# Turning the key-value product by VectorE and spreading it by small DMAs in a fused attention and FFN kernel

## The chip, the cores and the metric

The kernel runs on one core of a Trainium2 chip. The metric is the device time of one execution in microseconds, taken as the median of several runs. A profile of one execution shows what each engine did: TensorE (PE, with its weight loads as PEld), VectorE (DVE), ScalarE (ACT), GpSimd (POOL) and SyncE (SP), which issues most DMAs.

## The reference

Polynomial-sketch linear attention, then an FFN with a tanh-shrink activation. Four batches, four heads, 1088 tokens, head size 32.

```python
def phi(x):                                   # 32 -> 8 and 8 -> 64
    a = einsum('rd,bhsd->bhsr', S1, x)
    b = einsum('rd,bhsd->bhsr', S2, x)
    return einsum('bhsi,bhsj->bhsij', a, b).reshape(..., 64)
q_p, k_p = phi(q), phi(k)
kv  = einsum('bhsf,bhsd->bhfd', k_p, v)       # 64 x 32 per head
z   = sum(k_p, axis=2)
num = einsum('bhsf,bhfd->bhsd', q_p, kv)
den = einsum('bhsf,bhf->bhs', q_p, z)[..., None] + 1e-6
x   = (num / den) as (4352, 128)              # heads side by side
h   = x @ w_in                                # 128 -> 2048
out = (h - tanh(h)) @ w_out                   # 2048 -> 128
```

## The kernel before, in words

The attention works batch by batch. On the key side (`k_side`) the loaded keys are turned by VectorE (`kT`, L536), sketched by TensorE in 64x32 tiles (`ksk`, L581), turned back (`kab`, L593), multiplied out to 64 products per token (`w`, L648, on VectorE or GpSimd, three pieces a batch), and `kv_mm` (L663) sums products and values into one PSUM bank: `pv`, 128 partitions (head by 32 values) by 64 features. `gram` and `scmm` (L608, L618) give the denominators' weights.

The numerator (`num`, L818) wants kv the other way round, features on the partitions, and in all four partition quadrants, because it runs as 32x32 tiles: row quadrant g holds a quarter of the tokens, column quadrant h is a head, and the 64 features come in two halves x that are accumulated. `kv_tail` makes this so:

- `kvd`: a copy of pv to SBUF that repeats each half four times (128x256), on ScalarE or VectorE;
- `kvt`: two 128x128 transposes on TensorE (L681);
- `kvb`: a copy of the 128x256 result to SBUF, on ScalarE or VectorE.

Batch 0 has besides a quick path for its first 12 blocks (`kv_heads`, `q_heads`): a VectorE transpose of pv in 32x32 blocks (`kvh`, L691), a masked copy `kve` (L692) and two 128x128 matmuls (`num0.0`, `num0.1`, L737), whose casts to `xT` let the FFN begin.

The query side (`q_sketch` L759, `q_divide`, `q_piece`) does the like: sketch, transpose (`abc`, L764), denominators (`m`, `den`, `rd`, `aq`), products (`qp`, L802), transposes (`qpT`, L807), numerator, and two casts to `xT` (`x`).

The FFN takes `xT` in ten groups of columns (384, 352, 352, six of 512, 192). For each of 16 blocks of the hidden size: a matmul `h` (L923), a tanh on ScalarE (`th`, L927), for later groups an addition on VectorE (`dg`, L932), and a matmul `o` that sums into the output bank (L944). For the columns without `dg`, two matmuls with the product of both weights (`wch`, `wcl`, L948) supply the linear part. The output is turned by VectorE (`ot`, L953) and stored in four DMAs or more a group (`st`, L963). Three `ot` buffers take turns.

The order is written out by hand, or by a search: `TABLE` lists numbers of operations with a letter for the engine (v VectorE, a ScalarE, g GpSimd, t TensorE, s SyncE) and, after a colon, the buffer that a new value takes. Each engine runs its operations in that order and waits for semaphores of the operations that they depend on. F and f in the table are filler matmuls of 512 and 256 columns (L430, L429); they read a tile `zz` of zeros that VectorE fills first (L428). Operations marked `lock` take turns between VectorE and GpSimd. A large load waits until less than `CAP` bytes of earlier loads are on the way.

Of the kernel before, what the change touches and what calls it, by code (L numbers as in the profile page):

```python
# [19 lines left out]
CAP = 1.45e6  # L20
# [6 lines left out]
0v 15a 16s 18s 17s 56g 1g 10g 2g 14g 9g 13g 3g 6v 4v 5v 50v:0 12g 65g 58g 51v 54v 53v 52v 55g 7g 59g 19s 23s 22a 30s  # L27
21s F F F F F F F F F F F F 66t:0 84v 67t 69v:0 68t 70v F F F F f 71t:0 29s 20s 57g 8g 25s 72a:0 F f 73t 74a 24a 61g
27s 34s 64v 77v:0 76v:1 26s F F 85t:1 35s 78g:2 28s 107v 31s 75v 86v:0 87g:0 230a 88v:0 89v:0 90v:0 f 79t:0 80t 111t:0
81t 82v 33s F F F F F 238t:0 91v:0 92v:0 83g 229a 112v:1 42s 43s 32s 108a:0 95g:1 113g:0 96v:1 232g 40s 38s F f 237t  # L30
36s 39s 41s 114v:0 115v:0 f 109t f 93t:1 44s 37s 116g:0 239a 117g:0 119g:1 234g 231a f 97t:2 94v 110a:0 236g f 240t:0
124v:0 98a 45s 105s 100s 125v F 249t:1 250a:0 241t 253t:2 254a:1 251t:1 252a:2 233a 126t:0 255t:2 242v 48s 46s 257t:1
273t:0 128v:0 256a:3 281t:0 282t 283t 127v 279t:2 63g 129t:0 274a:4 259t:0 120v:0 258a:0 284t 261t:1 130v:0 118v 285t
280a:1 131t 243t:2 244t 99s 103s 101s 47s 102s 49s 104s 260a:2 262a:3 277t:0 263t:1 132v:0 121t:0 60g 133v 159v:0
278a:0 269t:0 160v 286t 136g:0 106s 264a:5 271t:1 235a 134v:1 123v 245t 122a 246t 270a:6 247a 161t:0 248v 135v:2
267t:0 265t:2 162v:1 272a:2 324t:1 266a:7 325a:8 62g 268a:9 137t:2 138t 139t 163v 169g:3 308t:1 170g:0 143v 140a:0
359t:0 309a:10 287t 288t 141t 360a:3 142a:0 316t:1 318t:2 317a:5 289t 275t:0 144t:0 178v 145v:0 146g:0 11g 147v:0
276a:7 319a:11 320t:1 290t 306t:0 291t 381t:2 292t 293t 321a:12 314t:1 307a:9 389t:0 382a:6 315a:2 294t 295t 304t:2
296t 390a:4 312t:1 305a:0 297t 298t 313a:7 299v:0 148v:0 332t:0 149v:0 164t:0 333a:1 165a:0 310t:2 311a:13 371t:1
336t:0 166t 367t:0 337t 328t:2 338t 339t 372a:0 167v:0 168v 322t:1 368a:14 329a:9 323a:10 179t:0 377t:0 330t:1 378a:13  # L40
150v:0 151v:0 326t:2 154g:1 327a:15 331a:16 340t 341t 342t 343t 152g:0 373t:0 374a:2 344t 387t:2 345t 180v:1 388a:5
334t:1 346t 335a:7 181g:0 347t 365t:0 348t 385t:2 366a:8 349t 386a:9 363t:1 350t 351t 352t 353t 369t:0 361t:2 155v
364a:1 153v 375t:1 376a:10 370a:7 362a:11 156t:0 383t:0 354v:1 379t:1 158a 391t:0 392t 182v:0 393t 157v 183v:0 394t
384a:12 430t:2 194v:0 380a:3 395t 418t:0 396t 431a:1 195v 414t:1 397t 444t:2 398t 399t 419a:8 400t 401t 436t:0 415a:0
402t 438t:1 403t 404t 184g:0 187v:0 213v 445a:2 432t:2 405t 406t 407t 408t 302s 437a:7 473t:0 439a:3 185g:1 433a:6
409v:2 428t:1 416t:2 171v:1 196t:0 474a:4 422t:0 446t:0 417a:5 429a:9 420t:2 434t:1 411s 172t:2 412s 197v:0 173t 198v
199t:0 174t 186v:0 189g:2 190v 205g:2 421a:10 424t:2 423a:0 435a:11 175a:0 200v:0 425a:12 447t 471t:0 472a:5 201t
440t:1 188v 176t 448t 426t:2 441a:13 357s 413s 410s 300s 489t:0 449t 450t 202v:0 203v 427a:8 490a:10 177v:0 442t:1
481t:2 214t:0 475t:0 451t 482a:0 443a:14 477t:2 206v:0 476a:15 452t 453t 487t:0 204v:1 478a:12 454t 499t:1 497t:2 455t
488a:8 456t 483t:0 457t 458t 215v:0 216v:0 217v:0 500a:9 218v:0 498a:16 469t:1 495t:2 459t 356s 219g:0 484a:1 485t:0  # L50
224v:0 225v:1 486a:6 470a:7 496a:11 191t:0 491t:0 222g:1 192v 220g:0 460t 493t:1 461t 462t 193a 524t:2 492a:17 463t
530t:0 223v 494a:3 479t:1 525a:13 464v:2 207t:0 465s 301s 531a:2 526v 208t 545t:2 501t:0 532v 536t:0 480a:14 527t:1
546a:18 221v 547v 537a:7 502t 503t 504t 538v 533t:2 505t 528a:5 506t 539t:0 529v 534a:4 507t 542t:1 540a:12 535v 508t
541v 543a:0 548t:2 509t 303s 510t 544v 560t:0 549a:1 511t 512t 554t:1 561a:14 550v 513t 562v 555a:6 551t:2 514t 552a:8
563t:0 515t 516t 556v 557t:1 517t 564a:10 518t 558a:3 553v 566t:2 567a:9 209t 565v 599t:0 600a:11 519v:0 572t:0 573t
559v 569t:1 570a:5 568v 602t:2 603a:13 358s 520s 467s 210v:0 601v 574t 523s 355s 575t 576t 571v 605t:0 577t 611t:1
578t 604v 606a:2 579t 608t:2 612a:4 607v 609a:0 211t 614t:0 615a:7 580t 613v 581t 617t:1 582t 610v 583t 616v 618a:12
620t:2 621a:1 584t 619v 623t:0 624a:6 212a:0 585t 586t 587t 588t 589t 626t:1 622v 625v 590v:1 635t:2 632t:0 226t:0
636a:3 627a:5 633a:8 637v 628v 641t:2 634v 629t:1 227a 647t:0 638t:0 648t 228v 649t 670t:0 671t 642a:9 639a:10 643v
675t:1 630a:2 644t:2 674t 640v 631v 650t 651t 652t 591s 466s 679t:2 593s 653t 678t 468s 672a:7 654t 655t 656t 657t  # L60
673v 682t:0 658t 683t 676a:8 677v 659t 686t:1 687t 660t 661t 645a:0 646v 702t:1 703t 680a:6 681v 691t:2 690t 522s 595s
521s 592s 684a:2 685v 704t 662t 688a:1 694t:0 695t 689v 692a:3 705t 663t 706t 699t:1 698t 597s 707t 708t 693v 730t:2
729t 664t 709t 710t 696a:5 697v 733t:0 734t 700a:4 701v 665v:0 596s 731a:6 598s 711t 712t 713t 669s 738t:1 737t 714t
715t 732v 735a:0 594s 736v 716t 717t 742t:2 741t 739a:1 718t 719t 740v 720v:2 745t:0 746t 667s 761t:0 762t 728s 750t:1
727s 743a:2 744v 749t 721s 668s 726s 722s 723s 666s 725s 747a:3 748v 763t 764t 765t 751a:4 753t:2 754t 766t 767t
757t:0 755a:0 758t 768t 769t 752v 724s 796t:1 770t 771t 772t 797t 756v 759a:1 798a:2 760v 773t 774t 784t:2 785t 786a:3
775t 791t:1 790t 776t 788t:0 792a:4 787t 803t:2 789a:0 802t 777t 778t 794t:1 793t 804a:5 808t:1 809t 799t:0 810t 800t
795a:1 801a:3 805t:2 806t 779v:1 780s 782s 807a:6 783s 811t 812t 813t 814t 815t 816t 781a 817t 818t 819t 820t 821t
822t 823t 824t 825t 826v:0 827s 829a 828s 830a
# [64 lines left out]
class _Prog:  # L134
# [40 lines left out]
    def plan(self, table, filler):  # L175
# [154 lines left out]
def bass_polysketch_attn__then__act_tanh_shrink_kernel(  # L330
# [24 lines left out]
    def pool(name, n, shape, dtype=FP32):  # L355
        return _singles([sb(name, shape, dtype) for _ in range(n)])
# [685 lines left out]
```

## Time and profile before

| | |
|---|---|
| median of 3 runs | 104.08 us (103.92 to 104.67) |
| profiled execution, its own time | 103.72 us |
| its span in the trace | 101.8 us |
| busy: PE, DVE, ACT, POOL | 97.0, 82.3, 80.1, 29.8 us |
| first FFN matmul starts | 17.10 us |
| FFN matmuls L923 and L944, share of the chain | 31% and 29% |
| fillers L430, share of the chain | 9% |
| loads from HBM | 8.95 MB, in the first third of the span |

The span is what the trace covers; some 1.9 us of the execution lie around it. A busy TensorE counts the modelled length of each matmul, which overlaps the next, so the distance between starts is what a matmul costs in a stream.

### The profile page before, as it was taken

How to read it: one execution, taken by the hardware profiler on the slowest of the kernel's cores; microseconds unless marked ns; L12 is line 12 of the kernel's file. 1: busy time of each engine (PE TensorE's matmuls, PEld its weight loads, DVE VectorE, ACT ScalarE, POOL GpSimd, SP SyncE). 2: the span in 40 equal slices, each digit the busy share in tenths (PEclk: the TensorE clock that was granted, in tenths of full speed). 3: DMA queues.
4: the chain of work that ended last, by engine and by line, in shares of the span. 5: the costliest groups of instructions: out<-in, count | busy, mean ns of one | idle time of the engine just before them, and what ended most of it. 6: DMA issues, size and time to landing. Idle time of an engine off the chain costs nothing.

```text
span 101.8 us, 3049 instructions
## 1 busy us (share of the span) xinstructions
PE 97.0 (95%) x1266; PEld 48.9 (48%) x1266; DVE 82.3 (81%) x148; ACT 80.1 (79%) x158; POOL 29.8 (29%) x50
## 2 busy tenths in 40 slices
PE   5999999999999999999999999999999999999960
PEld 2334666365744565554634454344453444444650
DVE  3449799699986996989998898688889788999530
ACT  0311257979799896998999799999979999989940
POOL 5130758963383292255501570000000000000000
PEclk9999999999999999999999999999999999999999
DMA  2898859999989300003400003106002640035445
GB/s 56 249 270 274 311 189 294 328 294 296 333 251 325 99 0 6 0 0 53 79 6 0 0 0 60 29 0 95 0 2 36 101 70 0 0 55 79 76 70 81
DMA packets 25917, 11.37 MB, mean 112 GB/s; under 512 B 19120, under 2 KB 23600, under 8 KB 25904
## 3 DMA queue, kind: packets, MB, share of 16 engines
q1 hardware_dynamic: 24528, 10.64, 40.6%
q10 hardware_dynamic: 1376, 0.54, 2.1%
q8 instruction: 10, 0.16, 0.7%
q14 instruction: 3, 0.02, 0.1%
HBM read 8.95 MB, written 2.23 MB: 110 GB/s over the span
## 4 chain that ended last, share of the span: by engine, by line
PE 95%; DVE 1%; ACT 0%; issue 0%
PE psb L923 31%; PE psb L944 29%; PE psb L430 9%; PE psb L818 6%; PE psb L663 5%; PE psb L581 3%; PE psb L948 3%; PE psb L759 3%; PE psb L737 1%; PE psb L608 1%; PE psb L901 1%; PE psb L429 1%; PE psb L681 1%; PE psb L706 1%; PE psb L887 1%; PE psb L618 1%
## 5 line engine op out<-in xcount | busy, mean ns | idle before, releaser
L927 ACT ACTIVATE th<-psb 128x512 bf16<-128x512 f32 (+3 forms) x135 | 70.3, 605 | 5.0 <-PE psb L923 4.3
L923 PE MATMUL psb<-xT,wi 128*128 128x512 bf16 (+3 forms) x160 | 47.3, 349 | 0.2 <-ACT th L927 0.2
L944 PE MATMUL psb<-th,wo 128*128 128x512 bf16 (+3 forms) x159 | 43.4, 347 | 0.0
L932 DVE TENSOR_TENSOR th<-psb,th 128x320 bf16<-128x320 f32 (+2 forms) x47 | 25.8, 558 | 4.5 <-ACT th L927 2.4
L923 PEld LDWEIGHTS psb<-xT,wi 128*128 128x128 bf16 x160 | 14.7, 98 | 22.8 <-ACT th L927 7.8
L944 PEld LDWEIGHTS psb<-th,wo 128*128 128x128 bf16 x159 | 15.3, 98 | 10.2 <-DVE ot L953 0.4
L802 POOL TENSOR_TENSOR qp<-ap,abc 128x768 f32<-128x768 f32 x8 | 12.0, 1511 | 6.9 <-DVE qp L802 5.4
L807 DVE STREAM_TRANSPOSE qpT<-qp 128x768 f32<-128x768 f32 x11 | 10.5, 962 | 0.2
L430 PE MATMUL psb<-zz 128*128 128x512 bf16 x26 | 9.3, 497 | 1.1 <-DVE zz L428 1.1
L648 POOL TENSOR_TENSOR w<-abk 128x768 f32<-128x768 f32 x5 | 7.5, 1517 | 8.4 <-DVE w L648 4.3
L953 DVE STREAM_TRANSPOSE ot<-psb 128x512 f32<-128x512 f32 (+3 forms) x10 | 6.2, 625 | 2.6 <-PE psb L944 2.6
L536 DVE STREAM_TRANSPOSE kT<-kL 128x576 f32<-128x576 f32 (+3 forms) x10 | 5.6, 600 | 1.4 <-DMA kL<-in_k_dram 1.4
L648 DVE TENSOR_TENSOR w<-abk 128x768 f32<-128x768 f32 x7 | 6.5, 947 | 0.1
L818 PE MATMUL psb<-qpT,kvb 32*32 32x288 f32 (+1 forms) x256 | 6.1, 392 | 0.0
L573 DVE STREAM_TRANSPOSE qT<-qL 128x1088 f32<-128x1088 f32 (+2 forms) x5 | 5.2, 1065 | 0.5 <-DMA qL<-in_q_dram 0.5
L663 PE MATMUL psb<-w,vL 128*32 128x64 f32 x288 | 5.4, 221 | 0.0
L764 DVE STREAM_TRANSPOSE abc<-psb 128x1152 f32<-128x1152 f32 (+1 forms) x4 | 5.0, 1262 | 0.4 <-PE psb L759 0.4
L663 PEld LDWEIGHTS psb<-w,vL 128*32 128x32 f32 x288 | 4.4, 110 | 2.0 <-issue 1.7
L430 PEld LDWEIGHTS psb<-zz 128*128 128x128 bf16 x26 | 2.8, 120 | 4.9 <-issue 3.1
L593 DVE STREAM_TRANSPOSE abk<-psb 128x288 f32<-128x288 f32 x8 | 3.4, 462 | 1.5 <-PE psb L581 1.5
L359 ACT ACT_TABLE_LOAD x1 | 1.3, 1283 | 4.2 <-DMA kL<-in_k_dram 4.2
L784 POOL TENSOR_TENSOR ap<-abc,rd 128x288 f32<-128x288 f32 (+1 forms) x3 | 1.9, 630 | 9.2 <-DVE rd L782 9.2
(90 smaller groups left out, 79.0 us busy)
## 6 DMA issues: line engine op xcount, KB each, us to landing
kL<-in_k_dram SPq DMA_DIRECT2D x8, 272.0 KB, 4.4
vL<-in_v_dram SPq DMA_DIRECT2D x15, 144.0 KB, 4.1
qL<-in_q_dram SPq DMA_DIRECT2D x6, 272.0 KB, 4.4
wo_f<-in_moe_w_out_dram SPq DMA_DIRECT2D x4, 256.0 KB, 4.1
out_dram<-ot SPq DMA_DIRECT2D x15, 64.0 KB, 2.0
wi_f<-in_moe_w_in_dram SPq DMA_DIRECT2D x3, 256.0 KB, 4.0
out_dram<-ot SPq DMA_DIRECT2D x8, 48.0 KB, 2.5
qL<-in_q_dram SPq DMA_DIRECT2D x2, 176.0 KB, 3.9
```

Of the source, the lines that this page charges most:

```text
L430: "F": lambda e, n: e.matmul(bank(3), zz.ap[:, 0:128], zz.ap[:, None, 128:384].to_broadcast([128, 2, 256]), start=True, stop=True)}, zop)
L536: P.add(_v(nb * 32 * (r1 - r0)), lambda e, n, e_=e_, nb=nb, r0=r0, r1=r1: e.transpose(kTv[b][r0].ap.rearrange("p (j u t r) -> p r j u t", ...
L648: P.add({**_v(768), **_gt(768)}, lambda e, n: e.tensor_tensor(out=wv.ap.rearrange("p (x i j) -> p x i j", i=8, j=8), in0=abh(0)[:, :, :, N ...
L663: i = e.matmul(pv[b].ap[h * 32:(h + 1) * 32, 0:64], vL[b][:, h, blk * 32:(blk + 1) * 32], wvs[b, p].ap[:, (bi * 4 + h) * 64:(bi * 4 + h + ...
L802: P.add({**_v(cn * 256), **_gt(cn * 256)}, lambda e, n, qp=qp, c0=c0, cn=cn: e.tensor_tensor(out=qp.ap[:, 0:cn * 256].rearrange("p (x i j) ...
L807: P.add(_v(cn * 256), lambda e, n, qp=qp, o0=o0, cn=cn: e.transpose(qt.ap[:, o0 * 256:(o0 + cn) * 256], qp.ap[:, 0:cn * 256]), r=[qp], w=[ ...
L818: i = e.matmul(psa4[h * 32:(h + 1) * 32, g, 0:nb * 32], kvb.ap[g * 32:(g + 1) * 32, x, h * 32:(h + 1) * 32], qq[g * 32:(g + 1) * 32, 0:nb, ...
L923: P.add(_mm(n_), lambda e, n, jb=jb, hv=hv: e.matmul(hv.ap[:, jb % m * 512:jb % m * 512 + n_], wi[jb // 4].ap[:, (jb % 4) * 128:(jb % 4 + ...
L927: act = P.add(_a(n_ * m), lambda e, n, hv=hv, th=th: e.activation(out=th.ap.rearrange("p (u x) -> p u x", u=m)[:, :, 0:n_], in_=hv.ap.rear ...
L932: P.add(_vp(gc * m), lambda e, n, hv=hv, th=th: e.tensor_tensor(out=th.ap.rearrange("p (u x) -> p u x", u=m)[:, :, 0:gc], in0=hv.ap.rearra ...
L944: fn = lambda e, n, x=x, st=st, sp_=sp_: e.matmul(ov.ap[:, 0:n_], wo[x // 4].ap[:, x % 4, :], ths[x][0].ap[:, ths[x][1] * 512:ths[x][1] * ...
L953: P.add(_vp(n_), lambda e, n: e.transpose(ot.ap[:, 0:n_], ov.ap[:, 0:n_]), r=[ov], w=[ot], name=f"ot{gi}")
```

## The change

1. `kv_tail` no longer copies, turns on TensorE and copies again. One VectorE instruction turns pv in 32x32 blocks straight into quadrant layout (`kvh1` to `kvh3`; batch 0 uses the transpose that its quick path has already). `kvb` of each batch has four slots; slot 0 is that transpose, in which quadrant h holds head h. Six DMAs from SBUF to SBUF a batch (`kvs`, 8 to 24 KB each) fill slots 1 to 3 with the same data, moved on by one, two and three quadrants. Tile (g, h) of the numerator reads slot (g - h) mod 4. A DMA may be issued by SyncE or ScalarE; in the new table ScalarE issues three of batch 0, SyncE all others.
2. Fillers read a constant of zeros that the program's preamble sets, spread by a zero step, so they depend on nothing. `zz` shrinks to 32 columns and is filled by GpSimd; only `gram0` reads it.
3. The 16 tiles of the numerator come in another order for each batch: diagonal (0), heads outermost as before (1), row quadrants outermost (2), heads outermost and reversed in the second half (3).
4. `CAP` rises from 1.45 to 2.0 million bytes.
5. `TABLE` is new on all engines. Among what moves: five of the `w` products from VectorE to GpSimd, `wqd` and a `wi` cast to GpSimd, both `qph` products to VectorE, the batch-0 q sketch behind the whole of `kvmm0`, `stt` ahead of the last `kT` of batch 0.

```diff
-CAP = 1.45e6
+CAP = 2.0e6
...
-    zz = sbv("zz", [128, 384], BF16)
-    zop = P.add({"vector": (1.0, 1.0)}, lambda e, n: e.memset(zz.ap[:, :], 0.0), w=[zz], name="zz")
-    filler = ({"f": ..., "F": ...}, zop)
+    zz = sbv("zz", [128, 32], BF16)
+    P.add({"vector": (120.0, 160.0), "gpsimd": (120.0, 160.0)}, lambda e, n: e.memset(zz.ap[:, :], 0.0), w=[zz], name="zz")
+    zc = nc.const_aps.tensor(0.0, [128, 1], FP32).bitcast(BF16)[:, 0:1]
+    fill = lambda n_: lambda e, n: e.matmul(bank(3)[:, 0:n_], zc.to_broadcast([128, 128]), zc.to_broadcast([128, n_]), start=True, stop=True)
+    filler = {"f": fill(256), "F": fill(512)}
...
     def kv_tail(b):
-        kvd, kvb = _Val(kvd_p), kvbv[b]
-        ...  kvd copy, kvt transposes, kvb copy
+        kvh, kvb = kvhv[b], kvbv[b]
+        if b:
+            P.add(_vp(64), lambda e, n: e.transpose(kvb.ap[:, 0, :], pv[b].ap[:, 0:64]), r=[pv[b]], w=[kvh], name=f"kvh{b}")
+        for r in range(1, H):
+            for j, (d0, s0, n_) in enumerate(((r * 32, 0, 128 - r * 32), (0, 128 - r * 32, r * 32))):
+                P.add({"sync": 480.0, "scalar": 400.0}, lambda e, n, r=r, d0=d0, s0=s0, n_=n_: e.dma_start(
+                    out=kvb.ap[d0:d0 + n_, r, :], in_=kvb.ap[s0:s0 + n_, 0, :]), r=[kvh], w=[kvb], dma=(n_ * 256, n_), name=f"kvs{b}.{r}{j}")
...
             for x in range(2):
-                for h in range(4):
-                    for g in range(4):
-                        i = e.matmul(psa4[h * 32:(h + 1) * 32, g, 0:nb * 32],
-                                     kvb.ap[g * 32:(g + 1) * 32, x, h * 32:(h + 1) * 32],
+                for i in range(16):
+                    u, w = i // 4, i % 4
+                    h, g = ((w, (u + w) % 4), (u, w), (w, u), (u if x == 0 else 3 - u, w if x == 0 else 3 - w))[b]
+                    r = e.matmul(psa4[h * 32:(h + 1) * 32, g, 0:nb * 32],
+                                 kvb.ap[g * 32:(g + 1) * 32, (g - h) % 4, x * 32:(x + 1) * 32],
```

In the new order, the entries of SyncE around batches 2 and 3 read (kvs: spreading DMAs, st: stores, lv: a load of v):

```text
st0.2, kvs2 x3, lv3.0, st0.3, kvs2, st2.3, kvs2, st2.0, kvs2, st1.3
kvs3 x2, st4.1, kvs3 x4, st4.3
```

More of the change, by code (lines that the diff above doesn't have):

```diff
@@ L32 @@
[L32 to L41, printed above, removed]
```

114 lines of the change are left out of this document (53 added, 61 removed).

## The prediction

> **What bounds the kernel now.** I read the page's slices and chain first, to see which engine sets the end, then the busy time by windows, then the chain in order of time, and last the timeline of the first 18 us.
>
> ```profile
> span 101.8 us, 3049 instructions
> ...
> PE   5999999999999999999999999999999999999960
> ...
> ACT  0311257979799896998999799999979999989940
> ...
> PE 95%; DVE 1%; ACT 0%; issue 0%
> ```
>
> ```profile
> 30.00:40.00 10.00, 9.96 (x147) 5.57 (x154) 8.86 (x14) 9.08 (x26) 4.70 (x6) 1.00 0.40 122
> ...
> 80.00:90.00 10.00, 10.00 (x50) 4.59 (x49) 9.27 (x13) 9.73 (x12) 0.00 (x0) 1.00 0.27 42
> ```
>
> After the stretch, the windows give busy time of PE, PEld, DVE, ACT, POOL. TensorE is busy in 9.96 and 10.00 of 10 us and carries 95% of the chain; ScalarE is second with 9.08 and 9.73. So from the first FFN matmul on, a microsecond of matmul work taken away is worth up to a microsecond, and VectorE or GpSimd work moved about is worth nothing unless it makes TensorE wait. The start is different: there TensorE's time is filler.
>
> ```profile
> 0.84 0.23 DVE zz L428
> 1.12 5.30 PE psb L430 x12
> 6.42 1.03 PE psb L581 x32
> 7.46 0.97 PE psb L430 x4
> ...
> 17.48 0.50 ACT th L927
> ...
> 22.48 1.22 PE psb L818 x59
> ...
> 27.95 0.22 PE psb L681 x2
> ...
> 34.45 0.70 PE psb L759 x32
> ...
> 71.41 0.22 PE psb L681 x2
> ...
> 71.94 0.27 PE psb L948 x2
> ...
> 75.27 1.53 PE psb L818 x63
> ...
> 78.20 1.08 PE psb L923 x5
> ...
> 98.41 0.38 DVE ot L953
> ```
>
> Columns: start, length, what. The twelve opening fillers take 5.30 us, 0.44 each; the four after the k sketch 0.24 each. So TensorE runs at half rate until about 7 us, and the sketch (L581) starts when the fillers end, not when its data is there:
>
> ```profile
> 4.72 0.24 DVE L542 STREAM_TRANSPOSE stt<-sin 128x64 f32<-128x64 f32 x1 [0.34 <-DMA sin<-in_S_dram]
> 4.89 0.76 DVE L536 STREAM_TRANSPOSE kT<-kL 128x256 f32<-128x256 f32 x2
> 5.23 0.24 POOL L545 TENSOR_TENSOR wab<-stt,mask 128x32 f32<-128x32 f32 x1
> 6.35 1.10 PE L581 MATMUL psb<-kT,wab 64*32 64x144 f32 x32
> 10.30 1.52 POOL L648 TENSOR_TENSOR w<-abk 128x768 f32<-128x768 f32 x1 [4.30 <-DVE w L648]
> 12.93 0.24 DVE L691 STREAM_TRANSPOSE kvh<-psb 128x64 f32<-128x64 f32 x1
> 13.60 1.49 SPq L465 DMA_DIRECT2D wo_f<-in_moe_w_out_dram  x3
> 17.10 0.34 PE L923 MATMUL psb<-xT,wi 128*128 128x384 bf16 x1
> ```
>
> Data is complete at 4.89 + 0.76 = 5.65; the sketch starts at 6.35.
>
> **The change part by part.** The sum is made against the profiled execution, 103.72 us (span 101.8, 1.9 around it). The runs' median, 104.08, stands 0.36 above it; I carry the difference over to the median.
>
> *Start.* A filler that reads a constant waits for no memset, so the first can start when zz's memset did, at 0.84, not 1.12: 0.28. The new order has eleven long fillers and a short one (half length) before the sketch, not twelve: 0.22 less at the half rate. Together 0.50, from 6.35 to 5.85. The lower bound on its start is data: with stt moved ahead of the last kT transpose, stt still waits for its load until 4.72, then 0.24 and half of 0.76 give 5.34, so the gain cannot pass 1.0; if something other than zz holds TensorE's first instruction, only 0.22 is left. I take 0.50. [...]
>
> From the sketch to the first FFN matmul I follow the new order by the rows. The sketch, the two products on VectorE, the one on GpSimd (1.52) and the last two parts of the kv product keep their distance: the batch-0 q sketch no longer stands between those parts, but two parts, not one, now follow GpSimd's product, and the two cancel. After the transposed kv (L691, 12.93) came qp, its transposes, kve, two numerators and two casts, up to 17.10; with both qp on VectorE and kve behind them I get the same 4.2 within 0.1. ScalarE also issues three small DMAs here, before the wiT copy; at 0.6 each (the load that ScalarE issues takes 607 ns, quoted below) they end before the copy's operands are there. So the 0.50 arrives at the first tanh, 17.48.
>
> *TensorE transposes.* kvt disappears for four batches. That of batch 0 lay among fillers: nothing. The three others (L681, the first and the last shown above) are 0.22 each on the bound engine: 0.66.
>
> ```profile
> L359 ACT COPY kvb<-psb 128x256 f32<-128x256 f32 x3 | 1.1, 382 | 0.0
> L359 ACT COPY kvd<-psb 128x256 f32<-128x256 f32 x3 | 1.1, 370 | 0.1
> L648 POOL TENSOR_TENSOR w<-abk 128x768 f32<-128x768 f32 x5 | 7.5, 1517 | 8.4 <-DVE w L648 4.3 <-DVE abk L593 3.3 <-DVE scx L628 0.8
> L648 DVE TENSOR_TENSOR w<-abk 128x768 f32<-128x768 f32 x7 | 6.5, 947 | 0.1
> L818 PE MATMUL psb<-qpT,kvb 32*32 32x288 f32 (+1 forms) x256 | 6.1, 392 | 0.0
> L932 DVE TENSOR_TENSOR th<-psb,th 128x320 bf16<-128x320 f32 (+2 forms) x47 | 25.8, 558 | 4.5 <-ACT th L927 2.4
> ```
>
> *Copies and products.* ScalarE loses 2.2 us of copies, VectorE two more copies; five of the 768-wide products move from VectorE (947 ns) to GpSimd (1517). Neither engine is on the chain; the cover is TensorE's FFN work. The place where the cover is thinnest is w1: its three products now run one after another on GpSimd behind qp and two casts, some 4.6 us, and the kv product of batch 1 stands about where the last is done. Between a gain of 0.2 (ScalarE late less often) and a loss of 0.5 I take 0.
>
> *Numerator order.* Batch 1 keeps its order; three change. The trace has two orders of 16 tiles: 32 matmuls of L818 take 1.53, 16 of L759 with rows outermost take 0.70. Two halves at 0.70 would be 0.13 better; two like the second half (0.83) 0.13 worse. Three batches: between -0.4 and +0.4; I take 0, as neither row is nearer. [...]
>
> *The spreading DMAs.* Six a batch, 8 to 24 KB, behind one VectorE transpose of 0.24, and the numerator waits for all six.
>
> ```profile
> out_dram<-ot SPq DMA_DIRECT2D x4, 8.0 KB, 2.3
> out_dram<-ot SPq DMA_DIRECT2D x4, 16.0 KB, 1.6
> ```
>
> ```profile
> L963 SPq DMA_DIRECT2D out_dram<-ot x45: 315/470/2009, 33.1 to 99.5; - x45
> ...
> DMA to landing us min/median/max: 1.5/1.9/3.5
> ```
>
> ```profile
> 76.23 6.19 SPq L963 DMA_DIRECT2D out_dram<-ot  x9
> ```
>
> ```profile
> L465 ACTq DMA_DIRECT2D vL<-in_v_dram x1: 607/607/607, 3.6 to 3.6; - x1
> ...
> DMA to landing us min/median/max: 2.8/4.0/5.3
> ```
>
> The last fence is of the loads (L465). No row shows an SBUF-to-SBUF DMA; the nearest are stores of the same size: 1.9 to land, and nine in succession take 6.19, of which one is the 2.01 maximum, so 0.52 each. Batch 0: the six go out by about 15, among loads that take at most 5.3 to land, so by 20.3; their numerator stood at 22.48 and moves to 21.9: hidden. SyncE stands still until the transposed kv is there, about 12.7, with wo, k2, q1 and v1 queued behind; before, the wo loads went out at 13.60, so nothing is lost, and the larger CAP lets one of them out ahead. Batch 1 has some 10 us. Batch 3: all six on SyncE with a store among them. After the kv product: a gate product on VectorE ahead (L932) 0.56, transpose 0.24, six issue steps 3.1, landing 1.9: 5.8, and some 0.2 for the product's last matmul to end: 6.0. TensorE has 29 matmuls of 0.216 (1.08 / 5) and a pair of 0.27 until the numerator: 6.5. Slack 0.5. Batch 2: 0.56, 0.24, nine issue steps (four other DMAs among the six) 4.7, landing 1.9: 7.4; cover 32 x 0.216 and a q sketch of 0.70: 7.6, and two small groups more. Slack 0.2 or a little over. I take 0, and keep as the upper end a 2.01 issue in each chain, 1.5 more than reckoned, so 1.0 and 1.3 of waiting; the lower end is 0, since nothing here can come out ahead of a copy that was already hidden.
>
> *Sum.* -0.50 - 0.66 = -1.16: 102.56 for the profiled execution, 102.9 for the median.
>
> **The rivals.** (1) The spreading is late for numerators 2 and 3, and the time is longer. Place: SyncE between kvh2, kvh3 and their last issue. For: nine steps in series, a slack of half a microsecond and less, a longest issue of 2.01 and a longest landing of 3.5. Against: medians. One such issue and landing in each chain cost 1.5 + 1.6 each, less the slacks: 2.6 + 2.9 = 5.5 at the worst; half of it, 2.7, gives 105.6. It is slower than no change by 1% from 2.2 us of waiting on, as the 1.16 has to be eaten first.
>
> (2) Half of the gain is lost in places of the new order: w1 late on GpSimd (0.5), one late numerator (0.5): 103.9. For: three dependent products in series, ScalarE at 9.7 of 10 at the end, where an earlier matmul only waits for a bank. Against: TensorE's full windows.
>
> (3) The change does not do what it says at the start: TensorE's first instruction is held by its own start, so the constant buys no time and only the shorter filler counts: -0.22 - 0.66, 103.2.
>
> [...]
>
> [...]
>
> **How the numbers follow.** A change of 1% (about 1.0 us) is what a measurement of this kernel tells from none: faster below 103.0, slower above 105.1. Forecast 102.9: 0.40, split by that border 0.30 and 0.10. Rival 1: 0.20, of which 0.15 slower and 0.05 between. Rival 2: 0.13, between. Rival 3: 0.07, between, but 0.02 of it below the border by scatter. Rival 4: 0.18. Rival 5 and unnamed mishaps: 0.02. Faster 0.50, same 0.33, slower 0.17. The forecast's own range is 102.1 to 103.6; for 8 in 10 it reaches to rival 4 below and into rival 1 above: 101.7 to 105.0.
>
> **What would show it.** Right: the sketch starts near 5.85 and the first tanh near 17.0; no L681; the numerators of batches 2 and 3 follow the matmul before them without a gap, with their last spreading DMA landed before; TensorE ends about 1.1 earlier than 98.4. Wrong: a weight load of the numerator that waits for kvb; a sketch still above 6.2; a numerator well off 1.53; windows after 30 us in which TensorE is busy for less than 9.9 of 10.

## The result and the profile after

The changed kernel is slower: 105.5 us median (104.8 to 107.91, 20 runs) against 104.06 (103.48 to 107.78, 20 runs) of the kernel before; ratio 1.013, 95% interval 1.0094 to 1.0166. The forecast was 102.9. The ratio leaves out the executions that lie some per cent above the others, which both kernels have. The profiled execution of the changed kernel took 106.16 us, with a span of 104.4 (before: 103.72 and 101.8), so it lies 0.66 above its median.

The page of the changed kernel, its slices and its chain:

```profile
PE   7989998999999998999999499999999999999940
...
PE 51%; SPq 22%; DMA 9%; ACT 6%; DVE 4%; issue 3%; DVEq 0%
PE psb L936 19%; PE psb L915 15%; SPq L462 11%; SPq L677 9%; PE psb L428 7%; DMA qL<-in_q_dram 5%; ACT th L919 5%; PE psb L810 5%; DMA kvb<-kvb 4%; PE psb L661 2%; PE psb L579 2%; SPq L955 2%; PE psb L940 1%; DVE ot L945 1%; DVE qT L571 1%
```

TensorE's share of the chain has fallen from 95% to 51%. SyncE's queue has 22% of it: its loads (L462, 11%) and, new, the spreading copies (L677, 9%), with another 4% for their landing. One slice of TensorE's row, the 23rd, has a 4 where there were nines.

The timeline of the changed kernel (start, length, engine, line, what; in brackets the idle time before it and what ended that):

```profile
5.77 1.05 PE L579 MATMUL psb<-kT,wab 64*32 64x144 f32 x32
...
17.01 0.87 ACT L919 ACTIVATE th<-psb 128x384 bf16<-128x384 f32 x2 [0.55 <-PE psb L915]
...
22.38 1.28 PE L810 MATMUL psb<-qpT,kvb 32*32 32x192 f32 x64
39.86 1.59 PE L810 MATMUL psb<-qpT,kvb 32*32 32x288 f32 x64 [0.31 <-DMA kvb<-kvb]
58.75 1.59 PE L810 MATMUL psb<-qpT,kvb 32*32 32x288 f32 x64 [1.53 <-DMA kvb<-kvb]
77.12 1.60 PE L810 MATMUL psb<-qpT,kvb 32*32 32x288 f32 x64
...
100.33 0.38 DVE L945 STREAM_TRANSPOSE ot<-psb 128x192 f32<-128x192 f32 x1 [1.26 <-PE psb L936]
```

The same numerators in the timeline of the kernel before:

```profile
22.41 1.28 PE L818 MATMUL psb<-qpT,kvb 32*32 32x192 f32 x64
...
39.13 1.60 PE L818 MATMUL psb<-qpT,kvb 32*32 32x288 f32 x64
...
56.54 1.60 PE L818 MATMUL psb<-qpT,kvb 32*32 32x288 f32 x64
75.20 1.60 PE L818 MATMUL psb<-qpT,kvb 32*32 32x288 f32 x64
```

Read as milestones, the two columns say where 2.6 us went. The sketch and the first tanh come 0.5 earlier, as forecast; by the numerator of batch 0 that lead is gone (22.38 against 22.41). From there to numerator 1 the changed kernel takes 17.48 against 16.72 (0.76 lost), to numerator 2 18.89 against 17.41 (1.48 lost, of which 1.53 is a wait for `kvb`), to numerator 3 18.37 against 18.66 (0.29 won), from there to the last `ot` 23.21 in both, and behind it 4.07 against 3.39 (0.68 lost).

A second profile of the changed kernel, taken further down, repeats this in part: numerator 0 stands 0.25 later than before, and then 0.19, 1.45 and 0.59 are lost at the same places and 0.28 won. So the 1.5 us at numerator 2 and the 0.6 at the end belong to the kernel; most of the 0.76 ahead of numerator 1, with its wait of 0.31 for `kvb`, belongs to that one execution.

The wait of 1.53 is what the windows show between 50 and 60 us; before, TensorE was busy for all of these 10 us. The changed kernel:

```profile
50.00:60.00 10.00, 8.42 (x127) 3.85 (x125) 7.51 (x11) 8.27 (x17) 7.40 (x7) 1.00 0.28 53
```

SyncE's part of the timeline, behind VectorE's transpose `kvh2`, shows why:

```profile
49.16 0.25 DVE L673 STREAM_TRANSPOSE kvb<-psb 128x64 f32<-128x64 f32 x1 [1.01 <-PE psb L661]
49.44 2.38 SPq L677 DMA_DIRECT2D kvb<-kvb  x3
51.86 0.60 SPq L462 DMA_DIRECT2D vL<-in_v_dram  x1
52.51 0.59 SPq L955 DMA_DIRECT2D out_dram<-ot  x1
53.14 0.53 SPq L677 DMA_DIRECT2D kvb<-kvb  x1
53.71 0.58 SPq L955 DMA_DIRECT2D out_dram<-ot  x1
54.34 1.95 SPq L677 DMA_DIRECT2D kvb<-kvb  x1
56.33 0.59 SPq L955 DMA_DIRECT2D out_dram<-ot  x1
56.95 0.49 SPq L677 DMA_DIRECT2D kvb<-kvb  x1
```

Ten issues one after another, the last at 56.95. The chain in order of time has the landing that follows it, up to numerator 2 at 58.75:

```profile
56.95 1.70 DMA kvb<-kvb
```

### The profile page after: what moved, and what is told of

It is laid out like the page before. It is cut to its first block, busy times and chain, and to the rows that moved or that the text cites. A ratio compares the mean times of both kernels' runs of the same rounds, so it can differ in the third digit from the quotient of the medians.

```text
span 104.4 us, 3053 instructions
## 1 busy us (share of the span) xinstructions
PE 94.9 (91%) x1245; PEld 47.6 (46%) x1255; DVE 77.5 (74%) x142; ACT 78.1 (75%) x152; POOL 37.9 (36%) x57
## 4 chain that ended last, share of the span: by engine, by line
PE 51%; SPq 22%; DMA 9%; ACT 6%; DVE 4%; issue 3%; DVEq 0%
PE psb L936 19%; PE psb L915 15%; SPq L462 11%; SPq L677 9%; PE psb L428 7%; DMA qL<-in_q_dram 5%; ACT th L919 5%; PE psb L810 5%; DMA kvb<-kvb 4%; PE psb L661 2%; PE psb L579 2%; SPq L955 2%; PE psb L940 1%; DVE ot L945 1%; DVE qT L571 1%
## 5 line engine op out<-in xcount | busy, mean ns | idle before, releaser
L915 PE MATMUL psb<-xT,wi 128*128 128x512 bf16 (+3 forms) x152 | 44.9, 347 | 0.5 <-issue 0.3
L924 DVE TENSOR_TENSOR th<-psb,th 128x192 bf16<-128x192 f32 (+2 forms) x48 | 26.3, 553 | 4.7 <-ACT th L919 2.5
L936 PEld LDWEIGHTS psb<-th,wo 128*128 128x128 bf16 x160 | 15.5, 99 | 10.3 <-DVE ot L945 0.2
L646 POOL TENSOR_TENSOR w<-abk 128x768 f32<-128x768 f32 x10 | 15.0, 1512 | 4.8 <-DVE w L646 3.3
L793 POOL TENSOR_TENSOR qp<-ap,abc 128x768 f32<-128x768 f32 x9 | 13.4, 1511 | 9.1 <-DVE qp L793 8.9
L428 PE MATMUL psb<-const-float32-0.0 128*128 128x512 bf16 (+1 forms) x29 | 9.9, 454 | 1.1 <-PEq L1019 0.8
L534 DVE STREAM_TRANSPOSE kT<-kL 128x512 f32<-128x512 f32 (+3 forms) x10 | 5.8, 600 | 1.6 <-DMA kL<-in_k_dram 1.6
L359 ACT CAST xT<-psb 128x192 bf16<-128x192 f32 (+3 forms) x6 | 2.9, 480 | 3.7 <-PE psb L810 3.4
L359 DVE CAST xT<-psb 128x576 bf16<-128x576 f32 (+2 forms) x4 | 2.8, 689 | 3.9 <-PE psb L810 3.9
L661 PE MATMUL psb<-w,vL 128*32 128x64 f32 x288 | 5.3, 221 | 0.0
L428 PEld LDWEIGHTS psb<-const-float32-0.0 128*128 128x128 bf16 x31 | 3.0, 114 | 4.7 <-issue 4.2
L661 PEld LDWEIGHTS psb<-w,vL 128*32 128x32 f32 x288 | 4.3, 110 | 1.9 <-issue 1.0
L810 PEld LDWEIGHTS psb<-qpT,kvb 32*32 32x32 f32 x256 | 3.3, 103 | 3.6 <-DVE qp L793 1.8
```

Of the source, the lines that this page charges most:

```text
L428: fill = lambda n_: lambda e, n: e.matmul(bank(3)[:, 0:n_], zc.to_broadcast([128, 128]), zc.to_broadcast([128, n_]), start=True, stop=True)
L646: P.add({**_v(768), **_gt(768)}, lambda e, n: e.tensor_tensor(out=wv.ap.rearrange("p (x i j) -> p x i j", i=8, j=8), in0=abh(0)[:, :, :, N ...
L661: i = e.matmul(pv[b].ap[h * 32:(h + 1) * 32, 0:64], vL[b][:, h, blk * 32:(blk + 1) * 32], wvs[b, p].ap[:, (bi * 4 + h) * 64:(bi * 4 + h + ...
L793: P.add({**_v(cn * 256), **_gt(cn * 256)}, lambda e, n, qp=qp, c0=c0, cn=cn: e.tensor_tensor(out=qp.ap[:, 0:cn * 256].rearrange("p (x i j) ...
L810: r = e.matmul(psa4[h * 32:(h + 1) * 32, g, 0:nb * 32], kvb.ap[g * 32:(g + 1) * 32, (g - h) % 4, x * 32:(x + 1) * 32], qq[g * 32:(g + 1) * ...
L915: P.add(_mm(n_), lambda e, n, jb=jb, hv=hv: e.matmul(hv.ap[:, jb % m * 512:jb % m * 512 + n_], wi[jb // 4].ap[:, (jb % 4) * 128:(jb % 4 + ...
```

## The experiments

Theory A at first: the loss is the place of the copies in SyncE's queue, with the rest of the gain lost in the new order. Its rival: copies cost wherever they stand, or the new order loses by itself. An edit of the order moves only what is named. All ratios are to the kernel before, on the same chip.

**The copies alone, in the old order.** Kernel before, with `kv_tail`, `kvb` and the numerator of the change:

```diff
-kvd1, kvt1, kvb1          (and 2, 3; batch 0 alike)
+kvh1, kvs1 x6             (kvs directly behind kvh in SyncE's queue)
```

> The kernel of before, in its own order and with its own loads and fillers, in which only the tail of kv is changed: the three-step tail (kvd, kvt, kvb) is gone for all batches, kvh stands where kvd stood, the six copies kvs stand right behind it (batch 0 split over SyncE and ScalarE as in the changed kernel, batches 1 to 3 all on SyncE), and the numerators read in the changed kernel's tile orders. Theory A (what costs is the place of the copies in SyncE's queue, behind stores and a load): six copies in a row take 6 x 0.6 us of issue and 2.4 us of landing, about 6.0 us behind kvh, and numerator 2 comes 7 us or more behind it, so nothing waits and the three kvt transposes are saved: 0.3 to 0.7 us faster than before, 103.4 to 103.8. Theory B (the copies are late wherever they stand): numerator 2 waits again for kvb, 1 us or more, and the time is 104.7 or above.

105.78 us, ratio 1.0144 (1.0089 to 1.0198): slower by as much as the whole change, which is theory B's number. So a loss of this size does not need the new order. Where it sits in this kernel is not told, since its profiled execution (107.69) is 1.9 above its median. Theory B's wait is not in that trace: no numerator waits for `kvb`, and numerators 1 to 3 are 36.06 apart (36.07 before). So the run does not show that the copies land too late here, and its loss stays open.

**The constant fillers alone.**

```diff
-fillers read zz, wait for its memset; 12 F, f
+fillers read the constant, wait for nothing; one f less
```

> The kernel of before in its own order; only the fillers multiply the built-in zero constant in place of the tile zz, and one half filler ahead of the first sketch is taken out. Nothing else differs. If the 0.5 us that the start gains lasts (theory A: it was lost on the way by the new order), the time is 103.5 to 103.7 against 104.06. If the stretch from 17 to 30 us is bound by something that does not start earlier, such as the loads (theory B), the first tanh comes 0.5 us earlier and the end does not: 104.0.

104.22 us, ratio 0.9999 (0.9969 to 1.003): nothing. Its timeline:

```profile
5.25 0.95 PE L580 MATMUL psb<-kT,wab 64*32 64x144 f32 x32
...
13.25 0.62 ACT L359 CAST wi<-wi_f 128x512 bf16<-128x512 f32 x1 [2.24 <-DMA wi_f<-in_moe_w_in_dram]
...
17.39 0.88 ACT L926 ACTIVATE th<-psb 128x384 bf16<-128x384 f32 x2 [0.43 <-PE psb L922]
```

The sketch starts 1.10 earlier than before (5.25 against 6.35), the first tanh 0.09 earlier (17.39 against 17.48). In between ScalarE waits 2.24 and 0.48 us for pieces of `w_in`. Theory B of this run holds in its number, and in its place more strongly than expected: already the first tanh is held, where the expectation had it 0.5 earlier.

**No copies at all**, in the changed kernel:

```diff
-for r in range(1, H): ... kvs
-kvb.ap[g * 32:(g + 1) * 32, (g - h) % 4, ...]
+kvb.ap[g * 32:(g + 1) * 32, 0, ...]
```

> The changed kernel without its 24 copies: the numerators read the tile kvh in place of all four rotated ones, so three of four head blocks get wrong operands; every matmul, shape and order stays. What the copies cost in all is the difference from the changed kernel. Theory A: the wait of 1.5 to 1.8 us at numerator 2 and 0.3 us at numerator 1 go, and with them SyncE's issues: 103.4 to 103.7 against 105.5. Theory B (the new order has slow places of its own, of which the wait at numerator 2 only hides one): 104.5 to 105.

103.58 us, ratio 0.9939 (0.9905 to 0.9972): theory A. The copies cost 1.9% in all, and all else in the change, with four kvt fewer, is worth 0.6%.

**The copies of batch 2 in front.**

```diff
-st0.2, kvs2 x3, lv3.0, st0.3, kvs2, st2.3, kvs2, st2.0, kvs2, st1.3
+kvs2 x6, ..., st0.2, lv3.0, st0.3, st2.3, st2.0, st1.3
```

> The changed kernel with one edit: in SyncE's queue the six copies of batch 2 stand in a row right behind the wait for kvh2, ahead of the load lv3.0 and of four stores that stood between them. Theory A: the last copy is issued about 3.6 us behind kvh2 in place of 7.8, lands near 55.5 us in place of 58.7, and numerator 2 follows TensorE without a gap near 57: 1.4 to 1.7 us faster than the changed kernel, 103.8 to 104.1. Theory B (the copies take as long as the queues and the memory let them, whatever their place): they land after 57.5 us and less than 0.7 us is won, 104.8 or above.

105.67 us, ratio 1.0104 (1.0062 to 1.0146): theory B's number, about 0.3 us under the changed kernel. The profiled execution (105.16) shows theory A's mechanism: the numerator no longer waits, 17.29 behind numerator 1 in place of 18.89. Then 0.4 us comes back, where TensorE waits for a load of v:

```profile
PE psb L661 <- DMA vL<-in_v_dram: 0.4, 1, 0.4
```

**Batch 0's copies behind the loads; and three batches moved.**

```diff
-lwo0, kvs0, lwo3, kvs0 x2, lwo1, lwo2, lk2.0
+lwo0, lwo3, lwo1, lwo2, kvs0 x3, lk2.0
```

> The changed kernel with one edit: in SyncE's queue the three copies of batch 0 stand behind the last load of w_out (lwo2) in place of among those loads, so that no load stands behind the wait for kvh0; the three copies on ScalarE stay. Theory A (the copies cost at the start, because a copy that waits for kvh0 at the head of SyncE's queue holds back the loads behind it): lwo3 to lk2 are issued up to 2 us earlier, as in the kernel without copies, the 25th tanh comes 0.5 us earlier or more, and the time is 104.5 to 105.0 against 105.5 to 105.7 of the changed kernel. Theory B (the copies cost by their issues on ScalarE, by their bytes, or only at numerator 2): 105.3 or above.

105.75 us, ratio 1.0117 (1.0062 to 1.0171): no gain that shows. Theory A of this run falls.

```diff
+kvs1 x6 behind lv2.2; kvs2 x6 behind kvh2; kvs0 as above
```

> The changed kernel with the copies of three batches moved in SyncE's queue: those of batch 0 behind the last load of w_out, those of batch 1 behind the last six loads that stood among them (lv2.2 the last), those of batch 2 in a row right behind kvh2. Theory A: no load waits behind a copy and no copy behind a store, so most of the 2.0 us that the copies cost by the run without them comes back: 103.6 to 104.3. Theory B (ScalarE's issues and the transfers themselves cost, or numerator 1 now waits for its later copies): 104.7 or above.

106.3 us, ratio 1.0152 (1.0103 to 1.02). A miss for theory A. Loads that are no longer held back behind copies of batches 0 and 1 are no gain that shows. It is no clean test, since lv3.0 now stands behind the copies of batch 2, as in the run with these in front.

**The kvt alone**, taken from the kernel before:

```diff
-P.add(_pe(260, 185.0), kvt, r=[kvd, ident], w=[pv[b]], ...)
-... kvb <- pv[b].ap[:, 0:256]
+... kvb <- kvd.ap
```

> The kernel of before without its four kvt transposes on TensorE: kvb is copied from kvd in place of from the transposed tile, so the numerators get the block as it was before the turn; all else stays. It prices the kvt alone. The sum of the prediction: three of them on the path at 0.22 us each, 0.66 us less: 103.5 to 103.8 against 104.06 to 104.33 (less 0.6 to 0.7 of it). The rival: TensorE has slack at those places, or something behind them sets the pace, and less than 0.3 us is won.

104.66 us against 104.66, ratio 0.9977 (0.9943 to 1.001): 0.24 us less by the ratio (0.6 less to 0.1 more), not 0.66, so the rival holds. Weight loads of TensorE around the place of `kvt3`, first in the kernel before, then without it:

```profile
71.03 0.35 PEld L681 LDWEIGHTS psb<-ident,kvd 128*128 128x128 f32 x2
71.54 0.10 PEld L923 LDWEIGHTS psb<-xT,wi 128*128 128x128 bf16 x1 [0.15 <-DVE th L932]
```

```profile
71.86 0.10 PEld L918 LDWEIGHTS psb<-xT,wi 128*128 128x128 bf16 x1 [0.49 <-DVE th L927]
```

Without the transposes the next FFN weight load waits 0.49 in place of 0.15 us for VectorE to give its bank back. From numerator 2 (56.86) to numerator 3 (75.52) this kernel takes 18.66, as before, and from numerator 0 to the last `ot` 75.98 against 76.00: in the traces all `kvt` together are worth 0.02. TensorE was busy for 59.96 of the 60 us from 31 to 91 in the kernel before, yet the cycle of first matmul, tanh, addition and bank had the slack: between 44 and 80 us its FFN weight loads wait 8.1 us for tanh and addition before, 9.0 without `kvt`.

**The changed kernel again**, unaltered:

> The changed kernel, unaltered, for a second profile on the chip of the other three. All theories: 105.3 to 105.8. If the 1.95 us issue ahead of numerator 2 was chance, the wait of TensorE at numerator 2 is near 0.5 us in this profile in place of 1.5 to 1.8, and what it is behind the kernel of before by then is the larger part of the loss; if it belongs to the order, the wait is 1.2 us or more again.

105.98 us, ratio 1.0137 (1.009 to 1.0185). Its numerator 2, and the issues of batch 2's copies in this profile (count, then least, median and longest ns):

```profile
58.43 1.59 PE L810 MATMUL psb<-qpT,kvb 32*32 32x288 f32 x64 [1.50 <-DMA kvb<-kvb]
```

```profile
L677 SPq DMA_DIRECT2D kvb<-kvb x6: 492/596/1891, 49.2 to 56.6; - x6
```

The long issue is no chance: it comes in both executions (1.95, 1.89), and so does the wait (1.53, 1.50). The traces of two other runs with this stretch of the queue unaltered have it at the same copy (batch 0's copies late: 1.98; the lower limit of loads, below: 1.96).

**Batch 2's copies and lv3.0 in front.**

```diff
-st0.2, kvs2 x3, lv3.0, st0.3, kvs2, st2.3, kvs2, st2.0, kvs2, st1.3
+lv3.0, kvs2 x6, ..., st0.2, st0.3, st2.3, st2.0, st1.3
```

> The changed kernel with one edit: the load lv3.0 and then the six copies of batch 2 in a row stand ahead of the stores that stood among them (the earlier run with the six copies alone in front lost 0.47 us again, because lv3.0 was pushed behind stores and the kv matmuls of batch 3 waited for it). Theory A (the wait at numerator 2 is 1.57 us in every execution, and it is the queue's order alone): from the 73rd to the 79th tanh 4.1 us in place of 5.7, from the 79th to the last 38.0, and the time falls by 1.4 to 1.6 us to 104.0 to 104.4, level with the kernel before. Theory B (what is won there is given back elsewhere, as the run with the copies alone in front showed in its median): 105.0 or above.

104.51 us, ratio 1.0004 (0.9967 to 1.0041): theory A, a little above its 104.0 to 104.4. By the ratios the order of one queue is worth 1.3%, and the kernel is level with before. Its timeline:

```profile
49.56 3.88 SPq L677 DMA_DIRECT2D kvb<-kvb  x6
53.49 4.71 SPq L955 DMA_DIRECT2D out_dram<-ot  x7
58.24 0.60 SPq L462 DMA_DIRECT2D vL<-in_v_dram  x1
...
57.27 1.60 PE L810 MATMUL psb<-qpT,kvb 32*32 32x288 f32 x64
60.83 0.88 PE L661 MATMUL psb<-w,vL 128*32 128x64 f32 x48 [0.34 <-DMA vL<-in_v_dram]
```

The numerator waits no more. But the kv product of batch 3 (L661) waits 0.34 us for v, though lv3.0 is out early: the late one is another, lv3.2, issued at 58.24 behind seven stores. What the expectation says of lv3.0 was wrong.

From numerator 1 to numerator 3 the traces take 36.07 us before, 37.26 and 37.24 in the two executions of the changed kernel, 36.14 with the copies alone in front and 36.07 here. So the place of the copies is worth 1.1 to 1.2 us in this stretch, and moving lv3.0 as well adds nothing that the traces show. Why the ratios of these two runs lie 1.0% apart (1.0104, 1.0004) is open; they were measured on different chips.

**The limit of loads in flight**, each way:

```diff
-CAP = 2.0e6      (changed kernel)
+CAP = 1.45e6
```

> The changed kernel with one number changed: at most 1.45 MB of loads in flight as before, in place of 2.0 MB; same order, same copies. Theory A (with more in flight the pieces of w_in share the memory with loads that are needed later, land 1 to 2.5 us later than before, and the second half of the first tanhs waits for them): the last piece of w_in lands near 14 to 15 us in place of 15 to 17, the 25th tanh comes 0.3 to 0.7 us earlier against the first, and the time is 104.8 to 105.3. Theory B (the limit does not matter there, or later loads now come late in turn): 105.5 or above.

```diff
-CAP = 1.45e6     (kernel before)
+CAP = 2.0e6
```

> The kernel of before with one number changed: 2.0 MB of loads in flight in place of 1.45. Theory A (more in flight delays the pieces of w_in): the last piece lands 1 us later or more, the first 24 tanhs take longer, and the time is 0.3 to 0.8 us above before. Theory B (the loss from 17 to 31 us belongs to the new order alone): within 0.2 us of before.

The changed kernel with 1.45 MB: 105.24 us, ratio 1.0062 (1.0026 to 1.0099), 0.7% under the changed kernel by the ratios, whose intervals just touch. The kernel before with 2.0 MB: 105.15 us, ratio 1.0062 (1.0023 to 1.0102). Theory A both times: the limit is worth about as much in either order. The loads of `w_in` on the pages of before, before with 2.0 MB, the changed kernel, and that with 1.45 MB (last number: us to landing):

```profile
wi_f<-in_moe_w_in_dram SPq DMA_DIRECT2D x3, 256.0 KB, 4.0
```

```profile
wi_f<-in_moe_w_in_dram SPq DMA_DIRECT2D x3, 256.0 KB, 4.8
```

```profile
wi_f<-in_moe_w_in_dram SPq DMA_DIRECT2D x3, 256.0 KB, 5.5
```

```profile
wi_f<-in_moe_w_in_dram SPq DMA_DIRECT2D x3, 256.0 KB, 4.3
```

The fourth piece, which ScalarE issues, takes 4.0, 5.9, 6.7 and 4.3. With the limit at 2.0 MB these loads take 0.8 to 2.4 us longer than at 1.45, and the ones that are needed first pay. How they pay is in the traces of the changed kernel, first with 2.0 MB, then with 1.45:

```profile
15.63 0.61 POOL L359 CAST wi<-wi_f 128x512 bf16<-128x512 f32 x1 [1.18 <-DMA wi_f<-in_moe_w_in_dram]
16.83 0.38 DVE L770 TENSOR_REDUCE den<-m 128x24 f32<-128x216 f32 x1 [0.81 <-POOL m L767]
18.23 0.19 PEld L579 LDWEIGHTS psb<-kT,wab 64*32 64x32 f32 x16 [0.55 <-DVE kT L534]
```

```profile
14.09 0.61 POOL L359 CAST wi<-wi_f 128x512 bf16<-128x512 f32 x1
15.84 0.38 DVE L770 TENSOR_REDUCE den<-m 128x24 f32<-128x216 f32 x1
17.40 0.18 PEld L579 LDWEIGHTS psb<-kT,wab 64*32 64x32 f32 x16 [0.17 <-DVE kT L534]
```

In the new order GpSimd casts the late piece and only then makes `m`; VectorE's `den` waits for `m`, `kT` stands behind `den`, and TensorE's sketch of batch 1 waits for `kT`. Numerator 0 stands at 22.38 with 2.0 MB and at 21.41 with 1.45 (22.41 before). The lower limit has its own price later: with it VectorE's `qT` waits for a load of q between 28 and 38 us.

```profile
DVE qT L571 <- DMA qL<-in_q_dram: 1.0, 1, 1.0
```

**Three edits together, and two limits.**

```diff
+lv3.0, kvs2 x6 in front; CAP = 1.45e6; st8.0 issued by ScalarE
```

> The changed kernel with three edits: lv3.0 and the six copies of batch 2 in a row ahead of the stores, 1.45 MB in flight, and one store of the last but one group (st8.0) issued by ScalarE in place of SyncE, so that SyncE has one issue less ahead of the last two stores. If the three act apart: 1.5 us less from the copies, 0 to 0.7 from the loads, 0.3 from the end: 103.2 to 103.9, faster than before by 0 to 0.8%. If the loads' limit gains nothing and the end stays: 104.2.

104.32 us, ratio 0.9965 (0.9929 to 1.0002): above the 103.2 to 103.9 of the expectation. The sum of the single prices by their ratios (1.3% and 0.7%) lies just inside the interval, so that they add up is neither shown nor excluded.

The second edit, on top of the moved load, copies and store:

```diff
-left = CAP - o.dma[0]
+left = (1.45e6 if o.name[:3] in ('lk0', 'lk1', 'lq0', 'lv0', 'lwi', 'lwo') else CAP) - o.dma[0]
```

> The changed kernel with lv3.0 and the six copies of batch 2 ahead of the stores, st8.0 issued by ScalarE, and the lower limit of 1.45 MB in flight for batch 0's loads, the weights and k of batch 1 alone; the later loads keep 2.0 MB. Theory A (the higher limit hurts the pieces of w_in only, the lower limit hurts q of batches 2 and 3 only): the first tanh near 16.6 us, no wait for q near 30 us, and the time is 0.6 to 1.0 us under the version with the higher limit: 103.3 to 103.8. Theory B (the early lead is lost again whatever the limit, since the stretch up to 36 us is bound by the loads' bytes): 104.2 or above.

104.18 us, ratio 1.0002 (0.9961 to 1.0044): theory B. By its median it lies 0.36 under before on its chip, by the ratio level: the two limits add nothing that can be told from none.

**Which copies carry the rest.** From the kernel with two limits: batch 0's copies behind lwo2, no copies in batch 0, no copies at all.

```diff
+kvs0 x3 of SyncE behind lwo2
```

> The kernel with two limits, in which besides SyncE's three copies of batch 0 stand behind the last load of w_out. Theory A (copies at the head of the queue that wait for kvh0 hold back loads that are needed by 30 us): 0.2 to 0.5 us faster than with them among the loads. Theory B (with the limit the loads are held back anyway): no difference within 0.3 us.

```diff
-for r in range(1, H):
+for r in range(1, H) if b else ():
```

> The kernel with two limits without the six copies of batch 0; its third numerator reads kvh for all four rotations, so part of batch 0's output is computed from the wrong operands, with the same matmuls in the same order. The difference from the kernel with them is the price of batch 0's copies. Theory A (that is where the 0.65 us sits, by SyncE's and ScalarE's issues at 12.5 to 16 us): 0.4 to 0.7 us faster. Theory B: within 0.2 us.

```diff
-for r in range(1, H): ... kvs
```

> The kernel with two limits without any of the 24 copies (every numerator reads kvh for all four rotations; same matmuls, same order): what is left if spreading cost nothing. By the run without copies and the higher limit (0.994 of before) and 0.4 to 0.7 us for the limit: 102.8 to 103.4. Theory A (batch 0's copies carry the price): within 0.2 us of the kernel that leaves out those alone. Theory B (copies of batches 1 to 3 carry it, by loads that stand behind copies of batch 1): 0.4 us or more below it.

Ratios 0.9988 (0.9948 to 1.0028), 1.0005 (0.9964 to 1.0047) and 0.9884 (0.9829 to 0.9939): theory B each time. Batch 0's copies cost nothing that shows; those of the other batches still cost 1.2%. In the run without batch 0's the kv product of batch 3 waits for lv3.2 as well, longer (1.07 us). From numerator 1 to 3 its trace takes 36.80 us, against 35.68 without any copies: there the whole price is that wait.

**The late load of v in front, and batch 1's copies behind the loads.**

```diff
+kvs1, lv3.0, lv3.2, then the stores and kvs2
```

> The kernel with two limits, in which both late loads of v of batch 3 (lv3.0 and lv3.2) stand right behind the copies of batch 1 in SyncE's queue, ahead of the first stores and of the copies of batch 2. Theory A (what is left of the copies' price is that load, which they push behind 57 us): TensorE no longer waits for v near 59 us, from the 73rd to the 85th tanh 7.3 us in every profile, and the time is 0.4 to 0.8 us under the kernel with two limits: 103.4 to 103.8, ratio 0.992 to 0.996. Theory B (the price sits in batch 1): no change beyond 0.2 us.

103.54 us, ratio 0.9962 (0.992 to 1.0003). Theory A: the wait is gone, and by the ratios about a third of the 1.2% with it, though the intervals overlap. From numerator 1 to 3 the trace takes 35.66, as without copies.

```profile
58.99 0.88 PE L661 MATMUL psb<-w,vL 128*32 128x64 f32 x48
```

```diff
+lv2.3, lv3.1, lk3.0, lv2.1, lk3.1, lv2.2, then kvs1 x6, lv3.0, lv3.2
```

> The kernel c1 with the six copies of batch 1 behind the last of the six loads that stood among them (lv2.2). Theory A: those loads are needed late and the copies of batch 1 land in time either way: within 0.3 us of c1. Theory B (loads that wait behind kvh1 cost): all loads are issued by 29 us in place of 36, and 0.3 to 0.6 us more is won. If numerator 1 then waits for its copies, 0.3 us or more is lost.

103.64 us, ratio 0.9958 (0.9922 to 0.9994): the same as the run before it, theory A, so loads behind batch 1's copies cost nothing that shows. It is the one version with copies whose interval lies under 1, and it does so by 0.0006, as the best of several: by the ratios, with the queue and the limit put right, it is 0.4% faster than the kernel before and 1.7% faster than the changed one. What is left between it and the run without copies (0.9884; the intervals overlap) is not settled; it is not in the stretch from numerator 1 to 3 (35.67 and 35.68).

The 0.68 that the changed kernel loses behind its last `ot` is not the copies' doing: the two traces without copies have 4.02 and 3.97 there, the kernel before 3.39 and that without `kvt` 3.27. It belongs to the new order; which of its moves makes it is open.

## Why the prediction was wrong

*Start, -0.50.* The numbers came out: sketch at 5.77 (forecast 5.85), first tanh at 17.01 (17.0). The first filler starts at 0.77, not 1.12, as reckoned. That the rest agrees is in part luck. The kernel without `kvt` has the start of before, and yet its sketch is 0.60 earlier than in the trace before and its first tanh 0.47 later (17.95):

```profile
1.12 4.50 PE L430 MATMUL psb<-zz 128*128 128x512 bf16 x12 [1.12 <-DVE zz L428]
5.75 0.95 PE L581 MATMUL psb<-kT,wab 64*32 64x144 f32 x32
```

The same twelve fillers take 4.50 in one execution and 5.30 in another, so only some 0.50 of the 1.10 of the fillers' run is theirs. That the clock makes the fillers slow, as "half rate" may be read, is not shown: 0.44 and 0.24 each are measured, and the windows have a granted clock of 1.00 from the start. In the second profile of the changed kernel the first tanh stands at 17.29.

The lead was worth nothing. The step that failed is that the sketch, its products and the numerators were followed to the first matmul, and not the casts of `w_in`, which wait for their loads. In the changed kernel the lead reaches the first tanh and is gone 1.2 us later, when the sketch of batch 1 starts (18.24, before 18.29), by the cast that waits 1.18 us; with the lower limit it lasts to numerator 0. The fillers alone leave the end where it was (ratio 0.9999 with a sketch 1.10 earlier). Rival 4, a time below the forecast, has 0.18 in the chances and sets the lower end of the 8-in-10 range, 101.7; no run shows a term that leads there: the lead of the start was worth nothing, and the numerators of batches 1 to 3 take 1.59 to 1.60 as before.

*Transposes, -0.66.* The step that failed is the rule that TensorE's busy time is worth up to its length because windows are full and TensorE has 95% of the chain. Measured 0.24 us, with 0 inside the interval, and in the trace 0: the next weight load waited for its bank instead (0.49 us in place of 0.15). The profile before had the row for it, weight loads that wait for VectorE's `th` (6.4 us in all):

```profile
L923 PEld LDWEIGHTS psb<-xT,wi 128*128 128x128 bf16 x160 | 14.7, 98 | 22.8 <-ACT th L927 7.8 <-DVE th L932 6.4 <-ACT xT L359 0.5
```

*The spreading DMAs, 0.* The step that failed is that the long issue was taken out of the row of stores (nine in 6.19) before the step was reckoned, and then left to the upper end: 0 where the prediction's own upper end for batch 2 was 1.3. Measured is a wait of 1.5. Reckoned for batch 2: nine issue steps of 0.52, 4.7. Measured: 49.44 to 56.95, 7.5, that is about 0.6 a step (the median of L677 is 596 ns) and two long ones: one among the first three, which take 2.38 where 1.8 would do, and the one of 1.95. At 0.62 from start to start nine steps would put the last issue at 55.0 and its landing at 56.7; TensorE is ready at 57.2 (58.75 less the wait). So by this estimate the slack was larger than reckoned, the step of 0.6 alone would have fitted into it, and the two long issues, 1.9 us more than plain ones, make the wait. Batch 3 had a slack and kept it: its numerator follows without a gap. Rival 1 had the place and the mechanism. That its 105.6 lies beside the measured 105.5 is luck: it halves waits at two numerators, where there was one wait, whole, and it counts the 1.16 as won, which was not. The landing, 1.9, was right where no load is on the way (1.7 to 1.8 in batch 3). Batch 0 was hidden, as forecast, though its copies (4.1 to 5.0) landed later than any store (4.0 at most in this profile):

```profile
L677 SPq DMA_DIRECT2D kvb<-kvb x3: 557/617/1157, 12.7 to 14.8; - x3
L677 ACTq DMA_DIRECT2D kvb<-kvb x3: 534/612/617, 12.7 to 13.9; - x3
DMA to landing us min/median/max: 4.1/4.6/5.0
...
L677 SPq DMA_DIRECT2D kvb<-kvb x6: 537/586/598, 70.9 to 74.6; - x6
DMA to landing us min/median/max: 1.7/1.8/1.8
```

These are the changed kernel's copies of batch 0, among loads, and of batch 3, among stores.

*CAP and the cast on GpSimd.* The prediction names the limit once, as something that lets a load out ahead. It costs 0.6 to 0.7% in either order, and in the new one it takes the lead of the start with it. No term of the sum had it, and no rival.

*The load behind the copies.* The prediction counted the copies' delay and not that of the loads and stores behind them: lv3.2 came late for the kv product of batch 3 as soon as the first wait was removed.

*Numerator orders, 0.* Right: 1.59 to 1.60 for 64 matmuls in batches 1 to 3, before and after. Batch 2, with row quadrants outermost, takes 1.59 like batch 1 with heads outermost: no run shows a loss by the order, for which rival 5 stands in the chances (0.02 with unnamed mishaps).

*Products to GpSimd, 0*: in the changed profile the weight loads of the kv product wait 0.4 us for such a product, before 0.3; not tested by itself.

*The end.* The 0.6 to 0.7 us that the new order loses behind the last `ot` was in no term and in no rival.

## What to carry over

A copy through a DMA queue cost its place in the queue here (ten issues in 7.5 us, a wait of 1.5): count every issue ahead of it at its measured length (0.6 us) with a long one (1.95) among them, and then look at what it pushes back. Do not take a full engine for a bound until the instruction behind the one that is removed has been shown to have its operands and its bank: without `kvt` it waited 0.49 us in place of 0.15. And the lead at the start lasted here only as far as the load that arrived last (1.10 us at the sketch, 0.09 at the first tanh, with the constant fillers alone): follow every engine that stands behind that load, not TensorE alone.

## What the runs showed of the hardware

In the changed kernel's trace a copy of 8 to 24 KB from SBUF to SBUF lands 1.7 to 1.8 us after its issue when only other copies and stores are on the way (batch 3), and after 4.1 to 5.0 among loads of 256 KB (batch 0). SyncE's three of batch 0 took 4.1 to 5.0, with loads of `w_out` in the same queue; ScalarE's three, in a queue that had one 256 KB load on the way (issued at 8.88, 6.7 to landing), took as long, 4.6 to 4.8. From 12 to 15.5 us the core's DMA engines moved 359 GB/s, from 70 to 77 us 35. What in the company of loads makes a copy late is not shown.

SyncE's issue of such a copy takes 0.6 us in the median (595 ns of 21 in the changed kernel), and now and then 1.1 to 2.0 (1.10, 1.16 and 1.95 there). The longest stood at the same copy in two executions of one kernel (1.95 and 1.89 us) and in two kernels with the same stretch of the queue (1.98 and 1.96). In the first of them a fetch of instructions (16 KB by the page, 0.16 MB in 10) lies in the same stretch, 54 to 56.6 us:

```profile
q8 instruction: 1, 0.02, 3.4%
```

That the fetch is its cause was not tried. Against it speaks that the other long issue of that chain, 1.1 us from 49.44 on, has no fetch while it lasts.
